# Three heads of attention probabilities held at once instead of two, their second parts written in place, and a head's sums issued two steps after its scores

## The chip, the cores and the metric

The kernel runs on one core of one Trainium2 chip. The metric is the time of one execution on the device, in microseconds (us). The core has five engines that work side by side, each through its own instructions in a fixed order: TensorE (PE in the profile; its weight loads are listed apart as PEld), VectorE (DVE), ScalarE (ACT), GpSimd (POOL) and SyncE (SP), which here issues all DMAs. An instruction that waits for a semaphore holds up whatever stands behind it on its engine.

## The reference

The kernel computes a block with two halves on x of 2048 tokens by 1024 channels, all in float32. The first half is attention with 32 heads of 32 channels over four segments of 512 tokens, with a memory M, z that is carried from segment to segment; the second half is an MLP over the token axis. Cut to what matters here:

```python
mod = (silu(c) @ w_mod)                       # six rows: sa, ca, ga, sb, cb, gb
h = layernorm(x) * (1 + ca) + sa
q, k, v = h @ wq, h @ wk, h @ wv              # 32 heads, 4 segments of 512
for s in range(4):
    logits = qs @ ks.T * scale + mask         # causal, inside the segment
    p = softmax(logits)
    a_dot = p @ vs
    a_mem = (phi(qs) @ M) / (phi(qs) @ z + 1e-6)
    o = g * a_mem + (1 - g) * a_dot           # g = sigmoid(beta), one per head
    M = M + phi(ks).T @ vs;  z = z + phi(ks).sum
x = x + ga * (o @ wo)
h = layernorm(x) * (1 + cb) + sb
x = x + gb * mlp_over_tokens(h)               # 2048 -> 3584 -> 2048
```

## The kernel before

Large products are made with operands split into a high and a low part (`split`, lines 117 to 124), and three matmuls per pair (high x high, high x low, low x high). The attention stage is the part that the change touches. Behind it come the output product (`product`, matmuls at line 795) and the MLP (`mix`, matmuls at line 925), which the change leaves alone.

**Units of work.** The attention is cut into 32 units `t`: a group of four heads and one segment. `its` orders them: segments 0 and 1 for all eight groups, then segments 2 and 3. A unit has four heads `h`, so there are 128 heads `n = 4 t + h` in all.

**Projection of a unit**, `project(t, piece)`, four pieces:

- Pieces 0 and 1 make k and v of two blocks of 128 tokens each (48 matmuls, line 194) in one of two PSUM banks "pj", and ScalarE copies them into `k32` (line 400) and `v32` (line 401), which have one buffer each. ScalarE also casts v from PSUM into the bfloat16 tile `vp` (line 406); after piece 1 VectorE makes the rest `r1 = v32 - vp` (line 408). `vp` has three buffers and is asked for in piece 0, where GpSimd sets its column of ones (line 404).
- Piece 2 transposes k (line 415), makes q (24 matmuls, line 202), splits both into `sg`, makes phi of q and k (`pq`, `pk`, with scratch tiles tagged "tmp" in two buffers), and SyncE stacks three heads' operands into `sk` by DMA (`stack`).
- Piece 3 stacks the fourth head, completes `vp` from `r1` (lines 442 and 443: a head's v now stands in three bfloat16 parts and a column of ones, 97 columns), and runs `memory(t)`: reading M, z (line 455) and updating them (line 465, which reads `v32`).

**A head** goes through three functions:

- `maxima`: four matmuls (line 483) in three PSUM tiles sx, sy, sz, which share the two banks "s1"; VectorE takes the masked row maxima of each (line 485). For two heads together they are transposed, negated, split and brought by DMA into the last rows of `sk` (lines 491 to 498).
- `scores`: four matmuls (lines 519, 522, 525, 526) in the two banks "s2" make the logits minus the maximum; ScalarE takes the exponentials into `p32` (128 x 1280 float32, two buffers; lines 520, 523, 527); GpSimd sets the upper triangle of the diagonal blocks to zero (line 530); ScalarE casts to the float16 first part (line 532), and GpSimd subtracts it for the float16 second part (line 534, two instructions). Both parts stand in one tile `ph`, two buffers.
- `values`: 20 matmuls (line 548), ten with the first part and 97 columns and ten with the second part and 65 columns, sum `p @ v` and the row sums in the one bank "pv"; VectorE (lines 551 to 555) and GpSimd (line 558) scale them and add the memory's share in `am`. After the fourth head `am` is transposed (line 563), copied (line 565) and stored to `oT` by DMA.

**The order of the work.** The loop at line 690 writes the steps `n` in program order: scores of head n, maxima of head n + 3, values of head n - 1, one piece of a projection about eight heads ahead, and the smaller jobs planned for that step.

```python
for n in range(-LEADS, 4 * NI + VL):
    at(scores, n)
    at(maxima, n + LEADS)
    at(values, n - VL)
```

When the program is built, a scheduler makes each engine's order from this: an earlier line has the higher priority, and an instruction that its simulated timeline finds not yet ready lets a later one pass. So matmuls of the projection, or of the output product near the end, stand between those of the heads. `tc.issue_after(ins)` forbids this in one place: what is written inside it, and runs on the engine of `ins`, stands behind `ins` in that engine's order. It adds no semaphore. `behind(n, engines)` (a helper that is already there) does so for the instructions kept in the dictionary `marks`.

Of the kernel before, what the change touches and what calls it, by code (L numbers as in the profile page):

```python
# [7 lines left out]
F32 = mybir.dt.float32  # L8
F32R = mybir.dt.float32r
F16 = mybir.dt.float16  # L10
BF16 = mybir.dt.bfloat16
AF = mybir.ActivationFunctionType
ALU = mybir.AluOpType
# [4 lines left out]
S, D, H, DH, F = 2048, 1024, 32, 32, 3584  # L18
P = 128
# [8 lines left out]
NV = 97  # L28
FT = F // P
LEADP, LEADS, NSK = 8, 3, 8  # L30
XB = 4
VL = 1
PHB = 2
P32B = 2
ML0 = 36
HB = 3
WO0 = 65
# [3 lines left out]
LEADS = 3  # L41


def attention_and_mlp(ctx, tc, x, wq, wkv, wo, beta, w1, b1, w2, b2, c, wm_a, wm_b, out):
# [335 lines left out]
    def project(t, piece):  # L380
# [6 lines left out]
        if piece in (0, 1):  # L387
# [11 lines left out]
                ps = two_tiles(first[half])  # L399
            A.copy(k32[:, 2 * half:2 * half + 2], ps[:, :, 0:128])  # L400
            A.copy(v32[:, 2 * half:2 * half + 2, 0:128], ps[:, :, 128:256])
            if half == 0:
                d["vp"] = b.tile([P, 4, 4, NV], BF16, tag="vp", bufs=3, name=f"vp{t}")
                G.memset(d["vp"][:, :, :, 0:1], 1.0)
                d["r1"] = pj.tile([P, 4, 4, 32], F32, tag="r1", bufs=1, name=f"r1_{t}")
            A.copy(d["vp"][:, 2 * half:2 * half + 2, :, 1:33], ps[:, :, 128:256].rearrange("p a (h e) -> p a h e", h=4))  # L406
            if half:
                V.tensor_tensor(d["r1"], v32[:, :, 0:128].rearrange("p a (h e) -> p a h e", h=4), d["vp"][:, :, :, 1:33],
                                op=ALU.subtract)
        elif piece == 2:  # L410
            k32 = d["k32"]
            d["sg"] = sg = pj.tile([P, 4, L], F32R, tag="sg", bufs=1, name=f"sg{t}")
            ps = bank("pj", 2, f"kps{t}")
            for i in range(4):
                T.transpose(ps[:, 128 * i:128 * i + 128], k32[:, i], ident)
            split(sg[:, 2:4], ps, A, V)
            if t:
                ps = bank("pj", 2, f"qps{t}")
                for k in range(NK):
                    q_chunk(w, hp[k], k, ps)  # L420
            else:
                ps = first[2]
            split(sg[:, 0:2], ps, A, V)
            if seg:
                r = pj.tile([P, L], F32, tag="tmp", bufs=2, name=f"rq{t}")
                A.activation(r, ps, AF.Relu, scale=-1.0)
                A.activation(r, r, AF.Exp, scale=-1.0)
                d["pq"] = pj.tile([P, L], F32, tag="pq", bufs=1, name=f"pq{t}")
                V.scalar_tensor_tensor(d["pq"], ps, 0.0, r, op0=ALU.max, op1=ALU.add)
            if seg < 3:  # L430
                r = pj.tile([P, L], F32, tag="tmp", bufs=2, name=f"rk{t}")
                kf = k32.rearrange("p a n -> p (a n)")
                A.activation(r, kf, AF.Relu, scale=-1.0)
                A.activation(r, r, AF.Exp, scale=-1.0)
                d["pk"] = pj.tile([P, 4, 128], F32, tag="pk", bufs=1, name=f"pk{t}")
                V.scalar_tensor_tensor(d["pk"].rearrange("p a n -> p (a n)"), kf, 0.0, r, op0=ALU.max, op1=ALU.add)
            for h in range(3):
                stack(t, h)
        else:
            stack(t, 3)  # L440
            vp, r1 = d["vp"], d["r1"]
            A.copy(vp[:, :, :, 33:65], r1)
            V.tensor_tensor(vp[:, :, :, 65:97], r1, vp[:, :, :, 33:65], op=ALU.subtract)
            memory(t)
# [28 lines left out]
    def maxima(t, h):  # L473
# [5 lines left out]
        for tiles in ((0, 1), (2,), (3,)):  # L479
            s = bank("s1", 2, f"s{'xxyz'[tiles[-1]]}_{t}_{h}")  # L480
            outs = [(i, s[:, 128 * i * (len(tiles) - 1):][:, 0:128 * i + 128]) for i in tiles]
            for i, o in outs:
                T.matmul(o, q[:, 128 * i:128 * i + 128], k[:, 0:128 * i + 128], start=True, stop=True)  # L483
            for i, o in outs:
                marks[4 * t + h - LEADS, "V"] = V.tensor_tensor_reduce(  # L485
                    o, o, mask[:, 384 - 128 * i:], 1.0, -3.0e38, op0=ALU.add, op1=ALU.max,
# [25 lines left out]
    def scores(t, h):  # L512
        d = st[t]
        n = 4 * t + h
        q, k = d["sk", h][:, 0], d["sk", h][:, 1]
        p32 = r_.tile([P, 1280], F32, tag="p32", bufs=P32B, name=f"p32_{t}_{h}")
        d["ph", h] = ph = r_.tile([P, 2, 1280], F16, tag="ph", bufs=PHB, name=f"ph{t}_{h}")
        b0 = bank("s2", 2, f"a0_{t}_{h}")
        T.matmul(b0, k[:, 0:128], q, start=True, stop=True)  # L519
        A.activation(p32[:, 0:512], b0, AF.Exp, scale=SCALE, bias=shift)  # L520
# [2 lines left out]
        A.activation(p32[:, 512:896], b1_[:, 0:384], AF.Exp, scale=SCALE, bias=shift)  # L523
        b2_ = bank("s2", 2, f"a2_{t}_{h}")
        T.matmul(b2_[:, 0:128], k[:, 384:512], q[:, 384:512], start=True, stop=True)
        T.matmul(b2_[:, 128:384], k[:, 256:384], q[:, 256:512], start=True, stop=True)  # L526
        A.activation(p32[:, 896:1280], b2_[:, 0:384], AF.Exp, scale=SCALE, bias=shift)  # L527
        for base, step in ((0, 512), (896, 128)):
            w = bass.AP(tensor=p32.tensor, offset=p32.offset + base, ap=[p32.ap[0], [step, 2], [1, 128]])
            G.affine_select(w, w, pattern=[[0, 2], [1, 128]], compare_op=ALU.is_ge, fill=0.0, base=0,  # L530
                            channel_multiplier=-1)
        marks[n, "A"] = A.copy(ph[:, 0], p32)  # L532
        for c in (slice(0, 640), slice(640, 1280)):
            marks[n, "G"] = G.tensor_tensor(ph[:, 1, c], p32[:, c], ph[:, 0, c], op=ALU.subtract)  # L534

    def values(t, h):
        pr, g, seg = its[t]
# [6 lines left out]
        for part, w in ((0, NV), (1, 65)):  # L544
            for i in range(4):
                for j in range(i + 1):
                    o = col[j](i)
                    T.matmul(pv[:, i, 0:w], ph[:, part, o:o + 128], d["vp"][:, j, h, 0:w], start=(n == 0),  # L548
                             stop=(n == 19), skip_group_check=True)
                    n += 1  # L550
        V.reciprocal(pv[:, :, 0], pv[:, :, 0])
# [45 lines left out]
    def at(f, n):  # L597
        if 0 <= n < 4 * NI:
            f(n // 4, n % 4)
# [90 lines left out]
    for n in range(-LEADS, 4 * NI + VL):  # L690
        at(scores, n)
        at(maxima, n + LEADS)
        at(values, n - VL)
        m = n + LEADP
        if 0 <= m + 4 < 4 * NI:
            t = (m + 4) // 4
# [448 lines left out]
```

## Time and profile before

| | us |
|---|---|
| median of the runs | 2234.29 |
| fastest run | 2233.22 |
| the profiled execution | 2231.97 |
| its span, first instruction to last | 2230.3 |
| the stretch from the first to the last probability sum (line 548) | about 108 to 1041 |
| busy in the span: TensorE | 2194.8 |
| VectorE | 1675.3 |
| ScalarE | 1136.8 |
| GpSimd | 721.0 |
| mean granted clock of TensorE, of full | 0.995 |

The times of single instructions come from the one profiled execution. A row of a group has the line, the engine and the operation, what is written and read (without buffer numbers), the shapes, the count; behind the first bar the busy time in us and the mean of one in ns; behind the second bar the time in us that the engine stood idle just before them, and what ended that idle time. Busy time is a union: matmuls overlap in the pipeline, so the mean times the count is more than the busy time. A row of the timeline has the start, the length in us, the engine, the line and the operation. A row of the waits has who waited for whom, the us in total, how often, and the longest.

### The profile page before, as it was taken

The page shows a single profiled execution, that of the slowest core. Times are in us where ns is not written, and L with a number is a line of the kernel's source. Part 1 is how long each engine was busy: PE and PEld are TensorE (multiplying, and loading weights), DVE is VectorE, ACT ScalarE, POOL GpSimd, SP SyncE. Part 2 cuts the span into 40 slices and gives each one's busy share as a digit, 9 for nine tenths or more (in the row PEclk, how much of TensorE's full clock was granted, in tenths as well). Part 3 has the DMA queues.
Part 4 walks back from the last instruction along what each step waited for, and adds up shares of the span by engine and source line. Part 5 has one row for each costly group of instructions (what it writes and reads, how often), then busy time and mean ns, then how long its engine had stood idle before and what let it go on. Part 6 is the DMA issues. An engine that isn't in the chain of part 4 may idle for free.

```text
span 2230.3 us, 38268 instructions
## 1 busy us (share of the span) xinstructions
PE 2194.8 (98%) x13786; PEld 1885.9 (85%) x13786; DVE 1675.3 (75%) x3762; ACT 1136.8 (51%) x2082; POOL 721.0 (32%) x831
## 2 busy tenths in 40 slices
PE   8999999999999999999999999999999999999999
PEld 5889898889989989888888888888888888888887
DVE  7677677766767777655858766888888886969687
ACT  5477777756666656645636533533334242424232
POOL 2176666656766767654001200033330000000000
PEclk9999999999999999999999999999999999999999
DMA  7657565697656566765654586655556541414134
GB/s 285 191 170 212 161 191 155 202 293 220 187 165 199 178 199 181 214 189 180 218 198 178 223 322 258 245 221 221 206 204 224 204 146 62 151 57 146 57 123 151
DMA packets 175185, 423.05 MB, mean 190 GB/s; under 512 B 17524, under 2 KB 71828, under 8 KB 166036
## 3 DMA queue, kind: packets, MB, share of 16 engines
q1 hardware_dynamic: 174996, 420.61, 57.4%
q8 instruction: 109, 1.79, 0.3%
q14 instruction: 80, 0.66, 0.1%
HBM read 244.62 MB, written 125.06 MB: 166 GB/s over the span
## 4 chain that ended last, share of the span: by engine, by line
PE 87%; DVE 5%; DMA 3%; ACT 2%; POOL 2%; issue 1%; SPq 0%; ACTq 0%; DVEq 0%; POOLq 0%
PE mx L925 47%; PE nps L194 12%; PE po L795 7%; PE qps L202 7%; PE pv L548 3%; PE a L519 1%; POOL ph L534 1%; PE sz L483 1%; PE sx L483 1%; PE rd L455 1%; PE a L522 1%; PE sy L483 1%; PE up L465 1%; PE a L526 1%; ACT ph L532 1%
## 5 line engine op out<-in xcount | busy, mean ns | idle before, releaser
L925 PE MATMUL mx<-bU,sp 128*128 128x512 f32 x2352 | 534.2, 389 | 0.9 <-DVE ac L932 0.9
L925 PEld LDWEIGHTS mx<-bU,sp 128*128 128x128 f32 x2352 | 441.4, 188 | 93.2 <-issue 1.3
L194 PE MATMUL nps<-wv,h 128*128 128x256 f32 x3072 | 437.2, 282 | 1.3 <-DVE h L124 0.7
L121 ACT CAST sp<-wr 128x384 fp32r<-128x384 f32 (+2 forms) x408 | 217.3, 545 | 432.7 <-PE mx L925 355.4
L534 POOL TENSOR_TENSOR ph<-p,ph 128x640 f16<-128x640 f32 x256 | 381.2, 1510 | 155.1 <-ACT ph L532 150.8
L925 PE MATMUL mx<-bA,sp 128*128 128x512 f32 x1764 | 430.5, 389 | 0.0
L194 PEld LDWEIGHTS nps<-wv,h 128*128 128x128 f32 x3072 | 404.6, 189 | 8.7 <-DVE h L124 2.0
L925 PEld LDWEIGHTS mx<-bA,sp 128*128 128x128 f32 x1764 | 331.2, 188 | 68.6
L124 DVE TENSOR_TENSOR sp<-wr,sp 128x384 fp32r<-128x384 f32 (+2 forms) x408 | 259.7, 647 | 29.1 <-ACT sp L121 28.8
L932 DVE TENSOR_TENSOR ac<-mx,ac 128x512 f32<-128x512 f32 x280 | 189.7, 686 | 83.9 <-PE mx L925 83.5
L202 PE MATMUL qps<-h,wq 128*128 128x512 f32 x768 | 200.5, 403 | 0.4
L532 ACT CAST ph<-p 128x1280 f16<-128x1280 f32 x128 | 160.9, 1259 | 41.7 <-POOL p L530 41.3
L795 PE MATMUL po<-wo,ots 128*128 128x512 f32 x768 | 179.8, 390 | 0.6 <-DVE x L798 0.6
L795 PEld LDWEIGHTS po<-wo,ots 128*128 128x128 f32 x768 | 143.6, 188 | 30.1 <-DVE x L798 0.9
L202 PEld LDWEIGHTS qps<-h,wq 128*128 128x128 f32 x768 | 143.9, 193 | 29.0 <-ACT vp L406 1.4
L925 PE MATMUL mx<-bB,sp 128*128 128x512 f32 x588 | 164.0, 389 | 0.0
L530 POOL TENSOR_SCALAR_AFFINE_SELECT p<-p 128x256 f32<-128x256 f32 x256 | 121.3, 484 | 103.1 <-ACT p L527 51.8
L548 PE MATMUL pv<-vp,ph 128*128 128x97 bf16 (+1 forms) x2560 | 142.0, 201 | 6.5 <-DVE red L555 3.1
L548 PEld LDWEIGHTS <-ph 128*128 128x128 f16 x2560 | 113.9, 98 | 28.1 <-issue 13.3
L925 PEld LDWEIGHTS mx<-bB,sp 128*128 128x128 f32 x588 | 110.4, 188 | 22.9
L485 DVE CUSTOM_DVE_ANT_0 sx<-sx,mask 128x128 f32<-128x128 f32 (+1 forms) x256 | 93.7, 366 | 41.8 <-PE sx L483 39.5
L932 DVE TENSOR_TENSOR cc<-mx,cc 128x512 f32<-128x512 f32 x140 | 94.9, 684 | 39.6 <-PE mx L925 39.3
(207 smaller groups left out, 3149.7 us busy)
## 6 DMA issues: line engine op xcount, KB each, us to landing
sk<-sg SPq DMA_DIRECT2D x384, 128.0 KB
wr<-in_w_dram SPq DMA_DIRECT2D x28, 1024.0 KB
wr<-in_w_dram SPq DMA_DIRECT2D x32, 768.0 KB
bstu<-ucd SPq DMA_DIRECT2D x28, 768.0 KB
wsp<-wv SPq DMA_DIRECT2D x32, 512.0 KB
rawm<-in_wm_b_dram SPq DMA_DIRECT2D x32, 512.0 KB
wv<-wsp SPq DMA_DIRECT2D x32, 512.0 KB
pcd<-cc SPq DMA_DIRECT2D x14, 1024.0 KB
```

The costliest lines, as they stand in the source:

```text
L121: last_hi[0] = A.copy(hi, src)
L124: return lo_eng.tensor_tensor(lo, src, hi.bitcast(F32), op=ALU.subtract)
L194: T.matmul(ps[:, aa], h[:, j, 128 * tt:128 * tt + 128], wt[:, i, o:o + 256], start=(n == 0), stop=(n >= 6 * NK - 2), skip_group_check=True)
L202: T.matmul(ps, wt[:, i, o:o + 128], h[:, j], start=(k + n == 0), stop=(3 * k + n == 3 * NK - 1))
L485: marks[4 * t + h - LEADS, "V"] = V.tensor_tensor_reduce(o, o, mask[:, 384 - 128 * i:], 1.0, -3.0e38, op0=ALU.add, op1=ALU.max, accum_out= ...
L530: G.affine_select(w, w, pattern=[[0, 2], [1, 128]], compare_op=ALU.is_ge, fill=0.0, base=0, channel_multiplier=-1)
L532: marks[n, "A"] = A.copy(ph[:, 0], p32)
L534: marks[n, "G"] = G.tensor_tensor(ph[:, 1, c], p32[:, c], ph[:, 0, c], op=ALU.subtract)
L548: T.matmul(pv[:, i, 0:w], ph[:, part, o:o + 128], d["vp"][:, j, h, 0:w], start=(n == 0), stop=(n == 19), skip_group_check=True)
L795: T.matmul(ps, os_[:, i, P * ct:P * ct + P], wop[ct, nh][:, j], start=(n == 0), stop=(n == 3 * NK - 1))
L925: T.matmul(ps, ops[q][:, i, P * k:P * k + P], b[:, j], start=(m == 0 and first), stop=(m == 3 * nk - 1), skip_group_check=True)
L932: V.tensor_tensor(d, ps, d, op=ALU.add)
```

## The change

Four things change together.

- The sums of a head move from one step behind its scores to two (`VL` from 1 to 2). They are also put, on TensorE, behind the last score matmul (mark "P") and the last matmul of the row maxima (mark "S") of the step in which they stand.
- `p32` has three buffers instead of two. The first part of the probabilities has a tile of its own, three buffers; the second part is written over the front half of `p32`, so `p32` stays taken until the head's sums are done, and no longer only until the second part is made.
- `vp` is asked for in piece 3 instead of piece 0. Its first part is cast once, from `v32`, instead of in two halves from PSUM, and `r1` is made there too.
- `r1` loses its own buffer and takes turns in the two of "tmp".

```diff
--- before.py
+++ after.py
@@ -29,9 +29,7 @@
 FT = F // P
 LEADP, LEADS, NSK = 8, 3, 8
 XB = 4
-VL = 1
-PHB = 2
-P32B = 2
+VL = 2
 ML0 = 36
 HB = 3
 WO0 = 65
@@ -399,14 +397,6 @@
                 ps = two_tiles(first[half])
             A.copy(k32[:, 2 * half:2 * half + 2], ps[:, :, 0:128])
             A.copy(v32[:, 2 * half:2 * half + 2, 0:128], ps[:, :, 128:256])
-            if half == 0:
-                d["vp"] = b.tile([P, 4, 4, NV], BF16, tag="vp", bufs=3, name=f"vp{t}")
-                G.memset(d["vp"][:, :, :, 0:1], 1.0)
-                d["r1"] = pj.tile([P, 4, 4, 32], F32, tag="r1", bufs=1, name=f"r1_{t}")
-            A.copy(d["vp"][:, 2 * half:2 * half + 2, :, 1:33], ps[:, :, 128:256].rearrange("p a (h e) -> p a h e", h=4))
-            if half:
-                V.tensor_tensor(d["r1"], v32[:, :, 0:128].rearrange("p a (h e) -> p a h e", h=4), d["vp"][:, :, :, 1:33],
-                                op=ALU.subtract)
         elif piece == 2:
             k32 = d["k32"]
             d["sg"] = sg = pj.tile([P, 4, L], F32R, tag="sg", bufs=1, name=f"sg{t}")
@@ -438,7 +428,12 @@
                 stack(t, h)
         else:
             stack(t, 3)
-            vp, r1 = d["vp"], d["r1"]
+            v = d["v32"][:, :, 0:128].rearrange("p a (h e) -> p a h e", h=4)
+            vp = d["vp"] = b.tile([P, 4, 4, NV], BF16, tag="vp", bufs=3, name=f"vp{t}")
+            r1 = pj.tile([P, 4, 4, 32], F32, tag="tmp", bufs=2, name=f"r1_{t}")
+            G.memset(vp[:, :, :, 0:1], 1.0)
+            A.copy(vp[:, :, :, 1:33], v)
+            V.tensor_tensor(r1, v, vp[:, :, :, 1:33], op=ALU.subtract)
             A.copy(vp[:, :, :, 33:65], r1)
             V.tensor_tensor(vp[:, :, :, 65:97], r1, vp[:, :, :, 33:65], op=ALU.subtract)
             memory(t)
@@ -480,7 +475,8 @@
             s = bank("s1", 2, f"s{'xxyz'[tiles[-1]]}_{t}_{h}")
             outs = [(i, s[:, 128 * i * (len(tiles) - 1):][:, 0:128 * i + 128]) for i in tiles]
             for i, o in outs:
-                T.matmul(o, q[:, 128 * i:128 * i + 128], k[:, 0:128 * i + 128], start=True, stop=True)
+                marks[4 * t + h - LEADS, "S"] = T.matmul(o, q[:, 128 * i:128 * i + 128], k[:, 0:128 * i + 128], start=True,
+                                                            stop=True)
             for i, o in outs:
                 marks[4 * t + h - LEADS, "V"] = V.tensor_tensor_reduce(
                     o, o, mask[:, 384 - 128 * i:], 1.0, -3.0e38, op0=ALU.add, op1=ALU.max,
@@ -513,8 +509,9 @@
         d = st[t]
         n = 4 * t + h
         q, k = d["sk", h][:, 0], d["sk", h][:, 1]
-        p32 = r_.tile([P, 1280], F32, tag="p32", bufs=P32B, name=f"p32_{t}_{h}")
-        d["ph", h] = ph = r_.tile([P, 2, 1280], F16, tag="ph", bufs=PHB, name=f"ph{t}_{h}")
+        p32 = r_.tile([P, 1280], F32, tag="p32", bufs=3, name=f"p32_{t}_{h}")
+        hi, lo = r_.tile([P, 1280], F16, tag="ph", bufs=3, name=f"ph{t}_{h}"), p32.bitcast(F16)[:, 0:1280]
+        d["ph", h] = hi, lo
         b0 = bank("s2", 2, f"a0_{t}_{h}")
         T.matmul(b0, k[:, 0:128], q, start=True, stop=True)
         A.activation(p32[:, 0:512], b0, AF.Exp, scale=SCALE, bias=shift)
@@ -523,15 +520,15 @@
         A.activation(p32[:, 512:896], b1_[:, 0:384], AF.Exp, scale=SCALE, bias=shift)
         b2_ = bank("s2", 2, f"a2_{t}_{h}")
         T.matmul(b2_[:, 0:128], k[:, 384:512], q[:, 384:512], start=True, stop=True)
-        T.matmul(b2_[:, 128:384], k[:, 256:384], q[:, 256:512], start=True, stop=True)
+        marks[n, "P"] = T.matmul(b2_[:, 128:384], k[:, 256:384], q[:, 256:512], start=True, stop=True)
         A.activation(p32[:, 896:1280], b2_[:, 0:384], AF.Exp, scale=SCALE, bias=shift)
         for base, step in ((0, 512), (896, 128)):
             w = bass.AP(tensor=p32.tensor, offset=p32.offset + base, ap=[p32.ap[0], [step, 2], [1, 128]])
             G.affine_select(w, w, pattern=[[0, 2], [1, 128]], compare_op=ALU.is_ge, fill=0.0, base=0,
                             channel_multiplier=-1)
-        marks[n, "A"] = A.copy(ph[:, 0], p32)
+        marks[n, "A"] = A.copy(hi, p32)
         for c in (slice(0, 640), slice(640, 1280)):
-            marks[n, "G"] = G.tensor_tensor(ph[:, 1, c], p32[:, c], ph[:, 0, c], op=ALU.subtract)
+            marks[n, "G"] = G.tensor_tensor(lo[:, c], p32[:, c], hi[:, c], op=ALU.subtract)
 
     def values(t, h):
         pr, g, seg = its[t]
@@ -545,7 +542,7 @@
             for i in range(4):
                 for j in range(i + 1):
                     o = col[j](i)
-                    T.matmul(pv[:, i, 0:w], ph[:, part, o:o + 128], d["vp"][:, j, h, 0:w], start=(n == 0),
+                    T.matmul(pv[:, i, 0:w], ph[part][:, o:o + 128], d["vp"][:, j, h, 0:w], start=(n == 0),
                              stop=(n == 19), skip_group_check=True)
                     n += 1
         V.reciprocal(pv[:, :, 0], pv[:, :, 0])
@@ -690,7 +687,8 @@
     for n in range(-LEADS, 4 * NI + VL):
         at(scores, n)
         at(maxima, n + LEADS)
-        at(values, n - VL)
+        with behind(n, "PS"):
+            at(values, n - VL)
         m = n + LEADP
         if 0 <= m + 4 < 4 * NI:
             t = (m + 4) // 4
```

## The prediction

> **What bounds the kernel now.** I read the page first, then the table of stretches, then the waits and groups of the attention stretch, then its timeline. The page's head gives the span and the busy rows; the two rows behind them are of the table of stretches: the attention stretch, in which all 2560 matmuls of the probability sums (L548) fall, and the fullest 50 us inside it.
>
> ```profile
> span 2230.3 us, 38268 instructions
> PE 2194.8 (98%) x13786; PEld 1885.9 (85%) x13786; DVE 1675.3 (75%) x3762; ACT 1136.8 (51%) x2082; POOL 721.0 (32%) x831
> ...
> 108.00:1041.00 933.00, 913.98 (x7951) 830.27 (x7950) 666.37 (x1965) 621.10 (x1128) 601.55 (x709) 0.99 0.65 194
> ...
> 700.00:750.00 50.00, 50.00 (x481) 47.05 (x478) 37.09 (x116) 34.14 (x62) 34.43 (x44) 1.00 0.66 201
> ```
>
> The columns are TensorE, its weight loads, VectorE, ScalarE, GpSimd, the granted clock, the DMA share, GB/s. The change touches nothing outside this stretch. In it TensorE is busy for 913.98 of 933 us, so 19.0 us are idle: 0.85% of the kernel. VectorE is at 71%, ScalarE at 67%, GpSimd at 64%; none of them is full. An edit that gives them air is worth only what TensorE waited for them. The clock is 0.99; one hundredth more or less, which the order of work may bring, is worth 9.3 us by itself.
>
> What did TensorE wait for? The groups of the stretch name it, the sums and the two matmul lines beside them:
>
> ```profile
> L548 PE MATMUL pv<-vp,ph 128*128 128x97 bf16 (+1 forms) x2560 | 142.0, 201 | 6.5 <-DVE red L555 3.1 <-POOL ph L534 2.0 <-ACT p L523 1.3
> ...
> L519 PE MATMUL a<-sk 98*128 98x512 f32 x126 | 55.6, 441 | 3.1 <-DMA sk<-nt 2.3 <-ACT p L523 0.5 <-ACT vp L406 0.3
> ...
> L483 PE MATMUL sy<-sk 96*128 96x384 f32 x121 | 44.1, 365 | 3.2 <-DVE mx L485 3.0
> ```
>
> The sums have 6.5 of the 19 us; the rest is in pieces of 3 us or less. The waits of the other engines in the same stretch are far longer (who waits for whom: us in total, times, longest):
>
> ```profile
> POOL ph L534 <- ACT ph L532: 149.5, 113, 3.7
> ...
> ACT p L520 <- POOL ph L534: 18.7, 16, 2.5
> ...
> POOL vp L404 <- PE pv L548: 13.2, 13, 3.2
> ...
> ACT v L401 <- PE up L465: 6.0, 6, 1.7
> ```
>
> A head's probabilities go ScalarE (exponentials, cast to the first part), GpSimd (mask, two subtractions to the second part), TensorE. The timeline of one head shows how tight this is:
>
> ```profile
> 499.71 2.79 POOL L534 TENSOR_TENSOR ph<-p,ph 128x640 f16<-128x640 f32 x2 [1.38 <-ACT ph L532]
> ...
> 502.07 0.58 PEld L548 LDWEIGHTS <-ph 128*128 128x128 f16 x11
> ...
> 502.93 0.34 PE L483 MATMUL sy<-sk 96*128 96x384 f32 x1
> ...
> 503.11 0.36 PE L548 MATMUL pv<-vp,ph 128*128 128x65 bf16 x6
> ...
> 503.30 0.48 PE L483 MATMUL sz<-sk 96*128 96x512 f32 x1
> ...
> 1025.52 0.93 PE L548 MATMUL pv<-vp,ph 128*128 128x97 bf16 x20
> ```
>
> GpSimd ends the second part at 502.50, and TensorE takes the last six sums at 503.11: just in time. The 20 sums go in pieces, and the last piece stands between the row maxima's matmuls sy and sz. Only some heads, as at 1025.52, have all 20 in one go.
>
> **The change part by part.** There are 128 heads and 32 projections. No matmul is added or removed.
>
> *One step more between scores and sums.* The sums of a head now come two steps behind its scores. A step lasts 933/128 = 7.3 us, and all that the sums wait for is then done a step before. The 6.5 us in front of L548 go: 2.0 and 1.3 surely; the 3.1 (VectorE's reduction of the head before, out of the one pv bank) because two heads' sums are now a step apart. I take 6.5, bounds 3.3 and 6.5. What is late next is the row maxima, below.
>
> *Sums in one piece.* In one piece 20 sums take 0.93 us, 119.0 us for 128 heads; the group's busy time is 142.0, so at most 23.0 us lie in broken blocks. Most of that overlaps with the matmul in front, since TensorE is busy there. Bounds 0 and 23; I take 4, an estimate nearer to nothing because the idle rows show little.
>
> *vp made from v32 in the last piece of a projection.* These are the groups that change place or go:
>
> ```profile
> L406 ACT CAST vp<-nps 128x256 bf16<-128x256 f32 x64 | 23.6, 390 | 0.4 <-PE pv L548 0.4
> ...
> L442 ACT CAST vp<-r 128x512 bf16<-128x512 f32 x32 | 20.4, 637 | 10.6 <-DVE r L408 10.3
> ```
>
> and, of the answer for line 408 alone, count, shortest, median and longest in ns:
>
> ```profile
> L408 DVE TENSOR_TENSOR r<-v,vp x32: 645/740/1934, 49.4 to 954.6; 128x512 f32<-128x512 f32 x32
> ```
>
> Two casts out of PSUM, 64 x 390 ns = 25.0 us, become one out of SBUF, for which L442 is the nearest row: 32 x 637 = 20.4. ScalarE gains 4.6 us, all beside TensorE. The projection's bank is free one cast earlier; TensorE waited for that cast 0.3 us at L519 and little elsewhere: I take 1.0. The wait of 13.2 us on GpSimd goes too (vp's slot is asked for three steps later, while the sums that free it come one later), worth nothing, since GpSimd has 36% free.
>
> Against this, v32 has one buffer, and its last readers are now a cast and a subtraction that formerly ran a piece or two earlier: 0.637 + 0.740 = 1.38 us. The next projection's copy into v32 waited 6 times, 6.0 us, for the memory matmuls that read it. If each of those waits grew by 1.38, ScalarE would stand 8.3 us more, and only part reaches TensorE, which has two projection banks. I take 1.0; bounds 0 and 8.3. In L408's row the slowest subtraction took 1.93 us beside a median of 0.74.
> The Trainium skill, SBUF — State Buffer, section "Who interferes with whom", says that a VectorE instruction with two SBUF inputs and a GpSimd instruction that reads SBUF exclude each other, the second waiting for the whole of the first; L408's spread agrees with this, and by that rule the moved subtraction may cost 1.2 us more, 38 us over 32 if every one met GpSimd, on VectorE and not on TensorE.
>
> r1 shares the two "tmp" buffers with two other temporaries whose readers are VectorE's; nothing on TensorE waits for it within a step. Below nothing: it frees no engine. I take 0.
>
> *Second parts in place, three buffers.* The subtraction keeps its count and shape, and reads and writes as many bytes; only the place of the result is new.
>
> ```profile
> L534 POOL TENSOR_TENSOR ph<-p,ph 128x640 f16<-128x640 f32 x256 | 381.2, 1510 | 155.1 <-ACT ph L532 150.8
> ```
>
> I keep the 1510 ns. The exponentials no longer wait for the subtraction two heads before (18.7 us of ScalarE), but for the second sums three heads before, which stand a step earlier on TensorE. TensorE's share of that old wait is the 0.5 at L519. I take 0; bounds 1 gained, 18.7 lost if the new wait takes the old one's size and all of it passes to TensorE.
>
> *Sums behind the scores and the row maxima of their step.* This is an order on TensorE alone, without a semaphore. What is queued behind: the sums, and on VectorE their reduction, which has a step to spare. But the sums were also filler: sy and sz wait until VectorE has reduced what stood in their bank.
>
> ```profile
> PE sy L483 <- DVE mx L485: 3.0, 4, 1.5
> ...
> PE sz L483 <- DVE mx L485: 1.7, 3, 1.3
> ```
>
> and from the groups by shape:
>
> ```profile
> L485 DVE CUSTOM_DVE_ANT_0 sy<-sy,mask 128x384 f32<-128x384 f32 x121 | 69.6, 575 | 19.8 <-PE sy L483 19.3
> L485 DVE DVE_READ_ACCUMULATOR2_ANT mx<- 128x1 f32 x485 | 67.8, 140 | 0.0
> ```
>
> A gap costs one reduction, 0.575 + 0.140 = 0.715 us. Of the four pieces of a projection two have 48 matmuls to put there and one 24 twice as wide; the fourth has only the reading and updating of the memory. TensorE waited 3.0 (sy) + 1.7 (sz) = 4.7 us for it; I let that double: +4.7, bounds 0 and the 46 of the rival below.
>
> *The end.* The last sums and the last stores of oT come a step later; SyncE's queue then has a step's stack loads ahead of a store, and only the product reads it. The output product's matmuls fill TensorE there, and its loads of oT follow behind; the row shows what covers it (27 matmuls, 6.39 us).
>
> ```profile
> 1033.76 6.39 PE L795 MATMUL po<-wo,ots 128*128 128x512 f32 x27
> ```
>
> Without that cover it would cost a step, 7.3 us. I take 0.
>
> Sum: -6.5 - 4.0 - 1.0 + 4.7 + 1.0 = -5.8 us. The profiled execution took 2231.97 us, 1.67 more than its span; the median of the runs, 2234.29, lies 2.32 above it. So 2226.2 for an execution like the profiled one, and about 2228 as a median.
>
> **The rivals.**
> *Nothing to be had.* TensorE takes the projections where it would wait, before and after, and the pieces only change places: 2234, chance 0.13. For it speaks the 98%, against it the 6.5 us that have a name.
>
> *The row maxima stand bare (slower).* Place: TensorE's queue at sy and sz. Price: 0.715 us a gap. The forecast holds 7 more gaps; from 9 more (5.8 / 0.715 = 8.1), of 256 (two a head), the kernel is slower than before. If each head of the fourth step, 32 heads, has both bare, that is 64 x 0.715 = 45.8 in place of 4.7: 2228 + 41 = 2269. For it: the sums do stand between sy and sz at 503.11. Against it: in the stretch from 700 to 750 TensorE has no idle time at all, projections included. Chance 0.22, mostly under 2258.
>
> *More is hidden in the busy time (faster).* Weight loads fill 830.27 of 933, 89.0%; in the fullest stretch 47.05 of 50, 94.1%. If whole blocks brought the stretch there, 933 x (1 - 0.890/0.941) = 50.6 us would go: 2184; half of it 2209. The other stretches hold other mixes, which speaks against the whole. Chance 0.13, of it 0.03 beyond 2%.
> The Trainium skill, Trainium Kernel Development and Optimization, section "Performance Expectations", says that matmul busy time is a bad measure of the distance to the peak, because matmuls are pipelined, and names the busy share of the weight loads as a good one; it speaks for this rival, and the rows agree that the two shares differ (98.0% and 89.0%).
>
> **How the numbers follow.** The forecast has 0.52, for 2214 to 2238: 2228 with one hundredth of the clock either way (9.3) and, downwards, another 5 of the broken blocks. The range reaches to 2204, past half of the hidden time and to all 23 us of broken blocks (2234 - 6.5 - 23), and to 2258, where about two thirds of the slower rival and the 18.7 of the buffers lie. By these shares it holds nearly 9 in 10. A measurement here tells about 2% from no change: below 2190 or above 2279. Faster by that: 0.03. Slower, by bare maxima and a late buffer together: 0.07. Within: 0.90.
>
> **What would show it.** Right: in the groups after, the sums' idle time near 0 and one piece of 20 as the rule in the timeline; GpSimd's wait for pv at vp's memset gone; ScalarE no longer waiting for the subtraction; the stretch's busy TensorE over 98%. The maxima's waits (sy, sz from VectorE) tell the slower rival: about 9 us by my forecast, over 40 by it. v32: ScalarE's wait at the copy into it, 6 us or up to 14. What would make it wrong: another order of the projections and their DMAs, which the build may choose anew once the sums are bound, so that pk, sk or the weights come late; then waits for DMA at the scores (2.3 us now) grow by tens of us.

## The result: 0.25% slower, inside the range and on the other side of zero

The changed kernel takes 2238.64 us in the median of its runs, the kernel before 2232.93 us in the runs beside it: a ratio of 1.0025, 95% interval 1.0017 to 1.0032. The forecast was 5.8 us faster; it is 5.6 us slower (0.0025 x 2232.93). The interval is 0.15% wide, so these runs can tell far smaller differences than the 2% that the prediction took for the limit. Three of the 44 executions took 3612.71 us or more (the changed kernel's at a clock of 0.556), and the ratio leaves them out.

The page of the changed kernel, its head, and the tables of stretches of both kernels for 60 to 1100 us, a window that holds the whole attention stage in both (the first fence is after, the second before, the columns as above):

```profile
span 2240.2 us, 38057 instructions
## 1 busy us (share of the span) xinstructions
PE 2190.2 (98%) x13786; PEld 1885.7 (84%) x13786; DVE 1663.9 (74%) x3762; ACT 1138.2 (51%) x2050; POOL 725.6 (32%) x831
...
60.00:1100.00 1040.00, 1005.34 (x8516) 915.69 (x8517) 719.51 (x2134) 665.51 (x1181) 613.10 (x718) 0.99 0.63 193
```

```profile
60.00:1100.00 1040.00, 1020.12 (x8551) 922.83 (x8552) 739.39 (x2153) 671.78 (x1227) 608.20 (x719) 0.99 0.64 195
```

TensorE's busy time fell by 4.6 us (2194.8 to 2190.2). Its idle time in the span rose by 14.5 us (2230.3 - 2194.8 = 35.5, now 2240.2 - 2190.2 = 50.0). Both together are the 9.9 us by which the span grew between these two profiled executions; the medians lie 5.7 us apart. All of the new idle time is in the attention: 1040 - 1020.12 = 19.9 us before, 34.7 after. In groups, after (lines 516, 519, 522 are score matmuls, 478 the row maxima, 545 the sums, 192 the projection):

```profile
L516 PE MATMUL a<-sk 98*128 98x512 f32 x128 | 57.9, 453 | 9.8 <-DMA sk<-nt 5.7 <-ACT p L520 1.7 <-ACT vp L437 0.9
L478 PE MATMUL sx<-sk 96*128 96x128 f32 (+1 forms) x256 | 54.2, 288 | 4.2 <-DMA sk<-sg 3.2 <-DVE mx L481 0.4 <-DVE rdd L452 0.3
L478 PE MATMUL sz<-sk 96*128 96x512 f32 x128 | 54.0, 422 | 1.3 <-DVE mx L481 0.7 <-DVE rdd L452 0.4
L478 PE MATMUL sy<-sk 96*128 96x384 f32 x128 | 46.4, 363 | 3.3 <-DVE mx L481 2.5 <-DVE rdd L453 0.5 <-DVE rdd L452 0.3
L519 PE MATMUL a<-sk 98*128 98x384 f32 x128 | 45.4, 355 | 1.9 <-ACT gaw L263 1.4 <-ACT p L524 0.4
L522 PE MATMUL a<-sk 98*128 98x128 f32 x128 | 31.1, 243 | 2.9 <-ACT p L517 2.9
...
L545 PE MATMUL pv<-vp,ph 128*128 128x97 bf16 x1280 | 80.4, 208 | 2.5 <-DVE red L552 2.3
...
L192 PE MATMUL nps<-wv,h 128*128 128x256 f32 x2948 | 406.1, 283 | 4.5 <-DVE sg L122 2.5 <-DVE pq L419 1.7 <-ACT wv L119 0.2
```

The sums' idle time fell from 6.5 to 2.5 us, as forecast in kind. But in front of the score matmuls it rose to 9.8 + 1.9 + 2.9 = 14.6 us. Before, these stood at 3.1 (line 519) and 0.2 (line 525). The largest part is at the first score matmul of a head, where the wait for a DMA grew from 2.3 to 5.7 us; the third, which waits for exponentials alone, went from 0.2 to 2.9:

```profile
L525 PE MATMUL a<-sk 98*128 98x128 f32 x128 | 32.2, 252 | 0.2 <-ACT p L520 0.2
```

The timeline of TensorE, after, shows one of the four waits at a head's third score matmul (line 522); the second fence has GpSimd, VectorE and ScalarE ahead of it:

```profile
582.85 0.35 PE L519 MATMUL a<-sk 98*128 98x384 f32 x1
583.03 1.09 PE L192 MATMUL nps<-wv,h 128*128 128x256 f32 x8
...
584.38 0.38 PE L405 MATMUL kps<-ident,k 128*128 128x128 f32 x2
585.49 0.33 PE L522 MATMUL a<-sk 98*128 98x128 f32 x1 [0.73 <-ACT p L517]
585.65 0.33 PE L523 MATMUL a<-sk 98*128 98x256 f32 x1
585.83 0.62 PE L545 MATMUL pv<-vp,ph 128*128 128x97 bf16 x10
586.28 0.47 PE L545 MATMUL pv<-vp,p 128*128 128x65 bf16 x10
```

```profile
580.80 1.40 POOL L531 TENSOR_TENSOR p<-p,ph 128x640 f16<-128x640 f32 x1
...
584.29 0.35 DVE L552 SCALAR_TENSOR_TENSOR red<-red,gate,pv 128x128 f32<-128x128 f32 x1
...
584.75 0.68 ACT L517 ACTIVATE p<-a,shift 128x512 f32<-128x512 f32 x1
```

The third score matmul needs the bank that the exponential of line 517 is still reading, and TensorE stands for 0.73 us. Right behind stand 20 sums of a head two steps back, and TensorE runs them without any wait of their own. GpSimd had ended that head's second part at 582.20, and VectorE had read out the bank of the sums at 584.64. So they could have filled this gap, but their place is behind the last score matmul.

### The profile page after: what moved, and what is told of

It is laid out like the page before. It is cut to its first block, busy times and chain, and to the rows that moved or that the text cites. A ratio compares the mean times of both kernels' runs of the same rounds, so it can differ in the third digit from the quotient of the medians.

```text
span 2240.2 us, 38057 instructions
## 1 busy us (share of the span) xinstructions
PE 2190.2 (98%) x13786; PEld 1885.7 (84%) x13786; DVE 1663.9 (74%) x3762; ACT 1138.2 (51%) x2050; POOL 725.6 (32%) x831
## 4 chain that ended last, share of the span: by engine, by line
PE 85%; DVE 6%; DMA 4%; ACT 3%; POOL 1%; issue 1%; SPq 1%; ACTq 0%; DVEq 0%
PE mx L923 47%; PE nps L192 11%; PE po L793 7%; PE qps L200 7%; PE pv L545 3%; PE a L516 1%; PE sz L478 1%; PE sx L478 1%; DMA sk<-nt 1%; PE sy L478 1%; PE a L519 1%; PE up L460 1%; PE srow L294 1%; PE a L523 1%; DMA sk<-sg 1%
## 5 line engine op out<-in xcount | busy, mean ns | idle before, releaser
L192 PE MATMUL nps<-wv,h 128*128 128x256 f32 x3072 | 425.1, 283 | 5.7 <-DVE sg L122 2.5
L531 POOL TENSOR_TENSOR p<-p,ph 128x640 f16<-128x640 f32 x256 | 377.2, 1474 | 115.6 <-ACT ph L529 110.9
L527 POOL TENSOR_SCALAR_AFFINE_SELECT p<-p 128x256 f32<-128x256 f32 x256 | 139.0, 548 | 134.5 <-ACT p L524 84.6
L923 PEld LDWEIGHTS mx<-bB,sp 128*128 128x128 f32 x588 | 110.4, 188 | 22.9
L481 DVE CUSTOM_DVE_ANT_0 sz<-sz,mask 128x512 f32<-128x512 f32 x128 | 88.8, 694 | 39.1 <-PE sz L478 38.4
L517 ACT ACTIVATE p<-a,shift 128x512 f32<-128x512 f32 x128 | 88.4, 690 | 50.3 <-PE a L516 43.8
```

The costliest lines, as they stand in the source:

```text
L192: T.matmul(ps[:, aa], h[:, j, 128 * tt:128 * tt + 128], wt[:, i, o:o + 256], start=(n == 0), stop=(n >= 6 * NK - 2), skip_group_check=True)
L481: marks[4 * t + h - LEADS, "V"] = V.tensor_tensor_reduce(o, o, mask[:, 384 - 128 * i:], 1.0, -3.0e38, op0=ALU.add, op1=ALU.max, accum_out= ...
L531: marks[n, "G"] = G.tensor_tensor(lo[:, c], p32[:, c], hi[:, c], op=ALU.subtract)
L923: T.matmul(ps, ops[q][:, i, P * k:P * k + P], b[:, j], start=(m == 0 and first), stop=(m == 3 * nk - 1), skip_group_check=True)
```

## The experiments

Each kernel was compared with the kernel before on the same chip. Names that begin with a_ are edits of the changed kernel, those with b_ of the kernel before. All compute the whole reference. The theories grew with the results, so they are numbered in the expectations: 1, the sums are gone as filler because they have a fixed place; 2, the late vp holds up ScalarE; 3, the order that the build makes moves the time by chance; 4, p32 is held too long; 5, the place of the sums relative to the scores decides; 6, a place behind two marks costs anywhere.

**First: which part loses?**

a_free takes the order away:

```diff
-        with behind(n, "PS"):
-            at(values, n - VL)
+        at(values, n - VL)
```

> The changed kernel without the order behind the scores and row maxima; two steps of distance, three buffers and the late vp stay. Theory 1 (the fixed place takes the sums away as filler, so that TensorE stands at the scores): the extra 15 us of idle TensorE in the attention go, idle time in the span falls from 50 to about 35 us, and the time to 0.997 to 1.000 of the kernel before. Theory 2 (the late vp holds up ScalarE and the copies that stand behind it): nothing changes, 1.002 to 1.003. Theory 3 (any new order of the build moves the time by a few tenths of a per cent, whatever the edit): anywhere from 0.997 to 1.005.

b_vp puts the late vp and r1 alone into the kernel before (the two hunks of `project` in the diff above).

> The kernel before with vp and r1 made in the last piece of a projection alone; one step of distance and two buffers stay. Theory 1: 0.999 to 1.001. Theory 2: 1.002 to 1.003, with ScalarE's waits and SyncE's waits for it grown as in the changed kernel. Theory 3: anywhere from 0.997 to 1.005.

b_behind puts the two marks and `with behind(n, "PS")` alone into the kernel before.

> The kernel before with the sums put behind the scores and row maxima of their step, one step of distance and two buffers as before. Theory 1: slower, 1.002 or more, since the filler goes here too and the sums have less time; I expect 1.005. Theory 2: 1.000. Theory 3: 0.997 to 1.005.

b_r1tmp is the kernel before with one tag changed:

```diff
-                d["r1"] = pj.tile([P, 4, 4, 32], F32, tag="r1", bufs=1, name=f"r1_{t}")
+                d["r1"] = pj.tile([P, 4, 4, 32], F32, tag="tmp", bufs=2, name=f"r1_{t}")
```

> The kernel before with r1 taking turns in the two tmp buffers instead of its own, nothing else: an edit that by itself should cost nothing. Theories 1 and 2: 0.9995 to 1.0005, idle time of TensorE within 3 us of the 35 before. Theory 3: the time moves by 0.1 to 0.3% all the same, and the idle time by several us, with waits at other places.

Measured: a_free 0.9983 (0.9974 to 0.9991), b_vp 1.0003 (0.9994 to 1.0011), b_behind 0.9993 (0.9985 to 1.0002), b_r1tmp 0.9986 (0.9977 to 0.9995). The order is the part that loses: without it, the rest of the change comes out 0.17% faster than before. The late vp costs nothing that can be measured, so theory 2 falls. a_free lies where theory 1 put it, though its idle time (22.6 us in the window) isn't below that of before. But two expectations of theory 1 failed: the order by itself, one step behind the scores, costs nothing (1.002 or more was expected of b_behind), and the innocent edit b_r1tmp did move the time. The build made a new order from it (4275 of TensorE's 13786 matmuls stand at another place in its list), and the time moved by 0.14%.

**Second: what is special about two steps?**

a_vl1 has `VL = 1` in the changed kernel. a_lo2 gives the second parts two buffers of their own:

```diff
-        p32 = r_.tile([P, 1280], F32, tag="p32", bufs=3, name=f"p32_{t}_{h}")
-        hi, lo = r_.tile([P, 1280], F16, tag="ph", bufs=3, name=f"ph{t}_{h}"), p32.bitcast(F16)[:, 0:1280]
+        p32 = r_.tile([P, 1280], F32, tag="p32", bufs=2, name=f"p32_{t}_{h}")
+        hi, lo = (r_.tile([P, 1280], F16, tag=g, bufs=m, name=f"{g}{t}_{h}") for g, m in (("ph", 3), ("lo", 2)))
```

a_P has `behind(n, "P")`, a_S has `behind(n, "S")`.

> The changed kernel with the sums one step behind the scores instead of two; three buffers in place, late vp and the order behind scores and row maxima stay. Theory 4 (p32 is now held until the sums, and the sums come last in a step two later, so the exponentials of head n+3 start only when the sums of head n end, and the scores, through their two banks, wait with them): the loop gets a step of air, idle time of TensorE falls from 50 to about 38 us in the span, 0.998 to 1.001. Theory 1 (the sums are missing as filler, wherever p32 stands): still 1.002 to 1.004. Theory 3 (a new order alone, width about 0.15% as the shared buffer of r1 showed): 0.9985 to 1.0015.

> The changed kernel with the second parts in a tile of their own, two buffers, and p32 back to two buffers that are free after the subtraction; two steps of distance and the order stay, and the three tiles take as much room as in the changed kernel. Theory 4: the exponentials no longer follow the sums at once (median distance 0.94 us in the changed kernel, over 3 us here), 0.998 to 1.001. Theory 1: 1.002 to 1.003 as the changed kernel. But the subtraction of head n+2 now waits for the sums of head n, which may cost GpSimd some of it.

> The changed kernel with the sums behind the scores of their step alone, free of the row maxima. Theory 4: the sums stand behind the last score matmul still, which waits for the exponentials by the banks, so most of the loss stays: 1.001 to 1.003. Theory 1: half of the loss, 1.000 to 1.001. Rival of the forecast, bare row maxima: the loss goes, 0.998 to 1.000.

> The changed kernel with the sums behind the row maxima of their step alone, free of the scores. Theory 4: the sums may pass the scores that wait for a bank, so p32 comes free earlier: 0.998 to 1.001. Rival of the forecast, bare row maxima: the loss stays, 1.002 to 1.003.

Measured: a_vl1 0.9993 (0.9984 to 1.0002), a_lo2 1.0027 (1.0019 to 1.0036), a_P 1.0027 (1.0015 to 1.0039), a_S 0.9967 (0.9954 to 0.9979). Theory 4 was right on a_vl1, but falls with a_lo2: its p32 is free right after the subtraction, and it is as slow as the changed kernel. a_P and a_S part the two marks. a_P has the very list of instructions of the changed kernel on every engine, so the mark on the row maxima changes nothing, and a_P is the changed kernel run once more. a_S, without the mark on the scores, loses nothing, and is faster than either of its expectations. The groups of a_S (lines as in the changed kernel) show the idle time at the scores back at 2.2 + 1.4 + 0.4 = 4.0 us:

```profile
L516 PE MATMUL a<-sk 98*128 98x512 f32 x128 | 55.3, 432 | 2.2 <-DMA sk<-nt 2.0
...
L519 PE MATMUL a<-sk 98*128 98x384 f32 x128 | 46.4, 363 | 1.4 <-ACT p L524 0.8 <-ACT gaw L263 0.6
...
L522 PE MATMUL a<-sk 98*128 98x128 f32 x128 | 33.6, 262 | 0.4 <-ACT p L517 0.4
```

and those of a_P have 6.3 + 1.6 + 2.1 = 10.0. The changed kernel had 14.6 in the same order, so one profile tells such a sum to a few us:

```profile
L516 PE MATMUL a<-sk 98*128 98x512 f32 x128 | 59.2, 463 | 6.3 <-DMA sk<-nt 3.4 <-ACT p L520 1.5 <-issue 0.8
...
L519 PE MATMUL a<-sk 98*128 98x384 f32 x128 | 45.5, 355 | 1.6 <-ACT gaw L263 1.5
L522 PE MATMUL a<-sk 98*128 98x128 f32 x128 | 31.6, 247 | 2.1 <-ACT p L517 2.1
```

The timeline of a_S shows a head as it can be: some of the sums stand in front of the third score matmul, and it has no wait for its bank.

```profile
567.39 0.39 PE L545 MATMUL pv<-vp,ph 128*128 128x97 bf16 x5
567.61 0.31 PE L522 MATMUL a<-sk 98*128 98x128 f32 x1
567.75 0.33 PE L523 MATMUL a<-sk 98*128 98x256 f32 x1
567.92 0.31 PE L545 MATMUL pv<-vp,ph 128*128 128x97 bf16 x3
```

**Third: does another place among the scores cure it?** a_P1S moves the mark "P" from the last score matmul to the second; a_P1 does that and drops "S"; a_P0 sets the mark at the first score matmul, without "S".

```diff
-        T.matmul(b1_[:, 0:384], k[:, 128:256], q[:, 128:512], start=True, stop=True)
+        marks[n, "P"] = T.matmul(b1_[:, 0:384], k[:, 128:256], q[:, 128:512], start=True, stop=True)
...
-        marks[n, "P"] = T.matmul(b2_[:, 128:384], k[:, 256:384], q[:, 256:512], start=True, stop=True)
+        T.matmul(b2_[:, 128:384], k[:, 256:384], q[:, 256:512], start=True, stop=True)
```

a_lo2_free is a_lo2 without the order. a_memset, and the three names that end in _ms, write the memset of vp's ones behind the cast instead of ahead of it.

> The changed kernel with one mark moved: the sums stand behind the second score matmul of their step (L519) instead of the last, and behind the row maxima as before. Theory 5 (the loss is the place of the sums: they used to fill TensorE inside a head's scores, where the third and fourth score matmuls wait for the exponentials to free a bank; behind the last score matmul they are ready at once and fill nothing): the sums return between the second and the third score matmul, idle time of TensorE in the span 33 to 36 us, 0.996 to 0.999. Theory 4 (p32 held by late sums): also better, but only where the sums end earlier. Theory 3 (order by chance): 1.0010 to 1.0040, about the changed kernel.

> The same without the row maxima: the sums behind the second score matmul alone. Theory 5: 0.996 to 0.999, since the row maxima showed no cost of their own. Theory 3: 1.0010 to 1.0040.

> The changed kernel without the order, and with the second parts in two buffers of their own and p32 in two. Theory 5: the buffers hardly matter, 0.997 to 0.9995, as with the second parts in place. Theory 4, in a weak form (buffers in place cost something by themselves): better than the one in place by 0.1% or more, 0.996 to 0.997.

> The changed kernel with the memset of vp's ones written behind the cast instead of ahead of it: an edit that by itself should cost nothing. Theory 5: the sums keep their place behind the last score matmul, so the loss stays, 1.001 to 1.004. Theory 3: a new order by chance, 0.9985 to 1.0040, and then the loss isn't the place of the sums.

> The sums behind the second score matmul and the row maxima, with the memset of vp's ones written behind the cast, an edit that costs nothing by itself. Theory 5 with order by chance on top (about 0.15% either way): 0.997 to 1.000, the 1.0016 was chance. Theory 6 (any fixed place behind scores and row maxima together costs, wherever among the scores): 1.001 to 1.003 again.

> The sums behind the row maxima alone, with the same costless edit. Theories 5 and 6: 0.996 to 0.9985, the sums stay inside the scores. Order by chance alone (theory 3): anywhere from 0.996 to 1.003.

> No order for the sums, with the same costless edit. Theories 5 and 6: 0.997 to 0.9995. Theory 3: 0.996 to 1.003.

> The sums behind the first score matmul of their step alone. Theory 5: they fill the wait in front of the third score matmul, 0.996 to 0.999. Theory 6: the same, since only one mark is set. Theory 3: 0.996 to 1.003.

Measured: a_P1S 1.0016 (1.0008 to 1.0025), a_P1 0.9987 (0.9979 to 0.9996), a_lo2_free 1.0009 (1.0001 to 1.0018), a_P0 1.0016 (1.0007 to 1.0026). The four kernels with the swapped memset have the same list of instructions on TensorE, VectorE, ScalarE and SyncE as the kernels they come from, so they are repeats of an order more than new orders. As such they agree: 1.0036 (1.0022 to 1.0051) for 1.0025, 1.0019 (1.0009 to 1.0028) for 1.0016, 0.9970 (0.9954 to 0.9986) for 0.9967, 0.9985 (0.9975 to 0.9995) for 0.9983. What an order of the build gives comes back; it is no noise of the runs.

All kernels in one table. "Idle" is TensorE's in the window from 60 to 1100 us, of one profile (1040 less the busy time). "Inside" is counted in the trace: how many of the 20 sums per step start between the first and the third score matmul of a head, a mean over heads 8 to 117.

| kernel | ratio to before | idle, us | inside |
|---|---|---|---|
| before | 1 | 19.9 | 10.1 |
| a_S | 0.9967 | 18.3 | 8.8 |
| a_S_ms | 0.9970 | 17.8 | 8.8 |
| a_free | 0.9983 | 22.6 | 9.7 |
| a_free_ms | 0.9985 | 21.0 | 9.7 |
| b_r1tmp | 0.9986 | 22.9 | 10.2 |
| a_P1 | 0.9987 | 24.2 | 9.0 |
| b_behind | 0.9993 | 23.3 | 8.4 |
| a_vl1 | 0.9993 | 23.5 | 6.8 |
| b_vp | 1.0003 | 25.9 | 11.1 |
| a_lo2_free | 1.0009 | 27.0 | 10.4 |
| a_P0 | 1.0016 | 23.4 | 12.0 |
| a_P1S | 1.0016 | 29.4 | 8.7 |
| a_P1S_ms | 1.0019 | 24.6 | 8.7 |
| changed kernel | 1.0025 | 34.7 | 1.7 |
| a_P | 1.0027 | 32.7 | 1.7 |
| a_lo2 | 1.0027 | 30.8 | 1.5 |
| a_memset | 1.0036 | 34.4 | 1.7 |

What follows: the four kernels whose sums stand in one block behind the last score matmul, two steps back, are the four slowest, with 31 to 35 us idle, and no other kernel has more than 29.4. But the changed kernel, a_P and a_memset are one order of TensorE three times, so these are two orders, the other being a_lo2, which has other buffers. Taking the mark on the scores away gains 0.58% (a_S), taking both away 0.42% (a_free), and 0.18% with the buffers of a_lo2 (a_lo2_free). So the changed kernel loses by the mark on the scores: a_S and its repeat show that. Whether it is by the place of the sums, or by the order that the build made around it, is not shown. The place is likely, since both orders with it are the slowest of thirteen. But other pairs, which have no such difference of place, lie apart too: 0.14% for b_r1tmp, 0.26% between a_lo2_free and a_free, which differ in the buffers alone, and 0.29% between a_P1S and a_P1, which differ in the mark on the row maxima.

How the place would cost time is open as well. If the sums were missed as filler where the scores wait for exponentials, those waits would tell the slow kernels from the fast. They don't. The changed kernel has 5.0 us of them (1.7 + 0.4 + 2.9), and a_P1, faster than before and with its sums inside, has 5.7 (0.8 + 2.2 + 2.7):

```profile
L516 PE MATMUL a<-sk 98*128 98x512 f32 x128 | 55.6, 434 | 3.5 <-DMA sk<-nt 2.4 <-ACT p L520 0.8 <-ACT gaw L263 0.2
L519 PE MATMUL a<-sk 98*128 98x384 f32 x128 | 45.6, 356 | 3.2 <-ACT p L524 2.2 <-ACT gaw L263 0.9
...
L522 PE MATMUL a<-sk 98*128 98x128 f32 x128 | 33.7, 263 | 2.7 <-ACT p L517 2.7
```

Nor do the waits for DMA: in the changed kernel TensorE has 8.9 us of them (5.7 at the first score matmul and 3.2 at sx), before 2.3, but a_vl1, no slower than before, has 8.5. The new idle time of the changed kernel is many small pauses, 48 in place of 26, for all kinds of reasons.

The same order is harmless at one step. A likely reason, not tested by itself, is that the sums of the head before aren't ready when their turn comes: other matmuls pass them, and 8.4 or 6.8 of 20 still slip into the next head's scores.

Three expectations of theory 5 failed. a_P1S and a_P0 were expected at 0.996 to 0.999 and came out at 1.0016, with their sums inside the scores, and a_lo2_free at 0.997 to 0.9995 and came out at 1.0009. Filling the scores is then not all of it. Theory 6 doesn't cover them either: a_P0 has one mark, and b_behind has two and costs nothing. a_P1S stands 4.4 us at the maxima for a stack's DMA and 3.8 us at the projection for a split, but in its repeat these are 2.4 and 2.1, and it is as slow; a_P0 has no single wait above 3.8 us, and little more idle time than before. Whether their marks cost, or the order that the build made around them, no run parts.

## Why the prediction was wrong

**The bound** was read rightly as far as it goes: none of the other engines was full, and in the profiles TensorE's idle time grew by more than its busy time fell. The idle time alone doesn't order the kernels, though: a_free has 22.6 us for 19.9 and is faster.

**One step more between scores and sums**: 6.5 us taken, 4.0 came (6.5 to 2.5). GpSimd's and ScalarE's share of the wait went. VectorE's, 3.1 us, which I had let go too, stayed at 2.3: the sums of two heads still share the one pv bank.

**Sums in one piece**: 4 us taken. Most blocks did become whole. The sums' own busy time fell from 142.0 to 122.1 us in the window (the second number of the row), near the 119.0 of the working:

```profile
60.00:1100.00 1040.00, 122.06 (x2560) 106.12 (x2560) 0.99 0.63 193
```

Most of these 20 us had overlapped with other matmuls, since TensorE's busy time fell by 4.6 us in all. Even that isn't shown to be a gain: the same order had 2190.2, 2195.2 and 2197.6 us busy in three profiles (the changed kernel, a_memset, a_P), and the kernel before 2194.8.

**vp from v32**: +1.0 for v32 and -1.0 for the bank. b_vp measured 1.0003 (0.9994 to 1.0011) for the two together, nothing. ScalarE's wait at the copy into v32, which I feared could grow from 6.0 to 14 us, fell:

```profile
ACT v L399 <- PE up L460: 3.2, 6, 1.1
...
ACT p L517 <- POOL p L527: 2.7, 5, 0.6
...
ACT p L517 <- PE pv L545: 2.4, 2, 1.8
...
POOL vp L434 <- PE pv L545: 0.8, 3, 0.3
```

The other rows are the waits that the buffers and the late vp were to take away: 18.7 us of ScalarE for the subtraction before, none of it left (2.7 for the mask, and 2.4 for the sums, the new wait that could have reached 18.7), and 13.2 of GpSimd before, now 0.8. Both went as forecast and were worth nothing, as forecast for engines that aren't full.

The moved subtraction has a median of 0.69 us and a longest of 1.90 us, like the 0.74 and 1.93 of before. The Trainium skill, SBUF — State Buffer, section "Who interferes with whom", would let it be longer beside GpSimd. The trace agrees: four of the 32 took 1.44 to 1.90 us, each beside a subtraction of GpSimd (line 531), and the other 28 at most 0.89. No wait of TensorE names the moved subtraction.

```profile
L436 DVE TENSOR_TENSOR r<-v,vp x32: 668/687/1901, 55.9 to 969.5; 128x512 f32<-128x512 f32 x32
```

**Three buffers in place**: 0 taken. a_lo2 against the changed kernel (1.0027 and 1.0025) agrees. Without the order the two layouts lie apart, 1.0009 (a_lo2_free) and 0.9983 (a_free), in favour of the buffers in place; whether the buffers or the order of the build did that, no run parts.

**Sums behind the scores and the row maxima** is the step that failed. It saw that the sums are filler, but priced only the row maxima, at +4.7 us; the mark on the scores it put at nothing, without a reason. At the row maxima the waits for VectorE's reductions fell, from 4.7 to 3.6 us (2.5 at sy, 0.7 at sz, 0.4 at sx), and a_P shows that the mark there changes nothing. The loss hangs on the mark on the scores: without it the kernel is at 0.9967, with it at 1.0025. In front of the scores 11.3 us of idle time came (3.3 to 14.6), and 8.7 more at sx and at the projection (0 to 4.2 and 0 to 4.5).

The nearest reading is that the sums were filler there too: before, 10.1 of 20 started between the first and the third score matmul, after it 1.7. But of the 11.3 us only 4.3 are waits for exponentials, which such filler would hide (0.7 to 5.0; at the third score matmul 0.2 to 2.9). 3.4 are waits for DMA, and a_P1 has as many waits for exponentials and no loss. So the step that failed is known, and how the place of the sums made the rest of the idle time stays open.

The rival "the row maxima stand bare" had the right sign, but its place, sy and sz, was not where the time went. "What would make it wrong" named waits for DMA at the scores; those grew from 2.3 to 5.7 us, and 3.2 came at sx, less than the tens that I wrote. The rival of hidden time fell with the sign: whole blocks came, but the weight loads' share of the span didn't rise (85% before, 84% after).

**The end of the stage** shows no cost. The last sums, of which the first fence has the second parts after and the second all of them before, start 15 us later; TensorE is busy all the time in between (third fence, after), with the output product, as the forecast said.

```profile
L545 PE MATMUL pv<-vp,p x1280: 190/193/262, 114.0 to 1055.5; 128*128 128x65 bf16 x183
```

```profile
L548 PE MATMUL pv<-vp,ph x2560: 190/204/278, 108.5 to 1040.7; 128*128 128x65 bf16 x99, 128*128 128x97 bf16 x98
```

```profile
1041.00:1060.00 19.00, 19.00 (x135) 15.70 (x135) 8.98 (x22) 5.17 (x8) 4.90 (x7) 1.00 0.46 152
```

## What to carry to other kernels

When an edit takes away a wait by giving work more slack, look where that work stood: on a full engine, work that was just in time may have been the filler of other waits, which then show little idle time. Price each place that it leaves, each mark by itself, and don't fix the place of what has become ready early without a run that leaves it free; here the same change without the mark on the scores (a_S, 0.9967, interval 0.9954 to 0.9979, one order of the build) is faster than both kernels. And where a build makes the order itself, innocent edits measure how much a new order does by chance; here one gave 0.14%, more than half of the effect in question, and one such sample doesn't bound it.

## What the runs showed of the hardware

In these traces a short stall of TensorE can be followed by a lower clock, and then costs twice: while it lasts, and behind it. The kernel before stood for 1.55 us ahead of 428.05 (first fence, its timeline); the stretches around it (second fence) show the granted clock at half for the 3.4 us that follow, in which TensorE is busy without a gap, and full again after.

```profile
428.05 0.44 PE L483 MATMUL sy<-sk 96*128 96x384 f32 x1 [1.55 <-DVE mx L485]
```

```profile
424.90:428.40 3.50, 1.95 (x26) 1.56 (x24) 3.50 (x12) 3.50 (x8) 3.49 (x4) 1.00 0.21 83
428.60:432.00 3.40, 3.40 (x14) 2.92 (x12) 3.40 (x12) 3.25 (x7) 1.68 (x2) 0.51 0.46 186
432.00:436.00 4.00, 4.00 (x29) 3.37 (x28) 1.99 (x2) 1.06 (x3) 3.23 (x2) 0.99 0.03 12
```

By estimate that is another 1.7 us of work (3.4 x 0.49). The Trainium skill, TensorE: Matmul & The Clock Gate, section "Part 1: The HAM clock gate (the "warmup" mystery)", gives half clock after an idle window of about 3.4 us; here it came after a stretch of 3.50 us in which TensorE was busy for 1.95. Nor is a long stall always there: from 124.9 to 131.7 us the clock of the kernel before was 0.50, with TensorE busy for 6.31 of the 6.80 us ahead of it; why, the trace doesn't show.

```profile
118.00:124.80 6.80, 6.31 (x55) 4.39 (x54) 6.56 (x29) 6.60 (x15) 4.20 (x6) 1.00 0.32 66
124.90:131.70 6.80, 6.56 (x28) 5.24 (x29) 4.32 (x11) 5.12 (x11) 5.62 (x8) 0.50 0.94 289
```

The mean clock over the runs was 0.996 for the kernel before and for the changed one, so it has no part in the loss between them, and 0.998 for a_S. The 0.0026 between 0.9956 and 0.9982 would be 5.8 us of 2233 if all of the time followed the clock, so a good part of a_S's gain of 7.4 us may have come through it, and 4.9 of the 13 us between a_S and the changed kernel (0.9960). By the same estimate a_free (0.9973, 3.8 us) and b_r1tmp (0.9980, 5.4 us) may owe the clock all that they gained (3.8 and 3.1 us).
